# An FNet block on one core: the second DFT later behind its operand's turn, SyncE's stores and loads moved, other addresses for Z's halves, a later last sum

## The chip, the core and the metric

The kernel runs on one core of a Trainium2 chip. The metric is the device time of one execution in microseconds (us), lower is better; it is the median of several runs. Engines are named as the profile names them: PE (TensorE, matmuls; PEld is its weight load), DVE (VectorE), ACT (ScalarE), POOL (GpSimd) and SP (SyncE, which in this kernel issues every DMA, in the order in which they are written).

## What is computed

Two sublayers with pre-normalization, on x of 2048 tokens by 448 channels, all in float32:

```python
x = A_x                                              # 1 x 2048 x 448
a = einsum("bsd,ed->bse", layernorm(x), dft_hid_re)  # DFT over channels
b = einsum("bsd,ed->bse", layernorm(x), dft_hid_im)
h = x + einsum("ts,bse->bte", dft_seq_re, a) - einsum("ts,bse->bte", dft_seq_im, b)
n = layernorm(h)
g, u = n @ w_gate, n @ w_up                          # 448 x 1792 each
out = h + (gelu(g) * u) @ w_down                     # 1792 x 448
```

## The kernel before, in words

Every float32 operand is split into two float16 halves (a high part, and a low part that is the rest), and each product is three matmuls: high by high, high by low, low by high. The high part is made on ACT (line 104), the low part on DVE (lines 108 and 110).

*The first stage: the DFT over the sequence.* The order of the two DFTs is turned round: the sequence comes first. For a pair p of token tiles (0 to 7, two groups g of 128 tokens, real and imaginary part), Z is a sum over 16 tiles of the normalized x, collected in PSUM banks acc (line 443). Pairs 0 and 1 run together in steps 0 to 15; from step 16 on each of the pairs 2 to 7 takes eight steps. A step n is 24 matmuls in all cases. `seq_load(n + 5)` loads raw DFT weights wr five steps ahead (lines 394, 399), and ACT and DVE make their halves ws three steps ahead.

*Z's way to the second DFT.* When a sum is done, `z_out` (line 453) makes its halves zs, two buffers, on ACT and DVE. `z_turn(p)` (line 462) issues four transposing DMAs on SP from zs to z, of which there is one buffer. `hid_mm(p, g)` (line 503) is the second DFT: 21 matmuls on z into y, in the one bank of the pool ps_tr, and then on DVE the sum of y into h, in the tile hx, which `h_tile` has filled with x. `h_store` writes hx to DRAM.

*What else goes on in that stage.* Pairs 0 to 3 of h are already made into operands of the next stage: moments and norm (`ffn_stats`, `ffn_norm`), sums (`ffn_sums`), halves xs, one buffer (`ffn_split`), and four transposing DMAs to hops (`ffn_transpose`, line 284). The gate and up weights are made into halves for 14 blocks f, one block every three steps: two loads into raw (two buffers, line 303), sums, two splits, and a store to DRAM (line 336).

*What sets the order.* All of this is written out by hand in two tables: `early[n]` holds what is issued in step n ahead of its matmuls, `after[n, half]` what is issued behind the first or the second half of step n's matmuls. Each engine takes its own instructions in the order in which they are written, and waits at the first one whose data or buffer isn't ready. So a store in SP's queue that waits for DVE holds back every load and every transpose written after it. In SBUF a new pool lies where a closed one was, and its tiles wait for what last used the addresses.

*The second stage: gate and up.* It opens when the last Z is done. Its pool fpool lies where the first stage's tiles were. A block t of `GateUp` has three banks X, Y, Z; `open` makes X and Y, from X ACT makes u1 (line 809), DVE u2 from Y and u1, and so on (`plus`, line 781). The last turn, z of pair 7, is issued in front of the stage, and `hid_mm(7, g)` runs at the ends of blocks 2 and 3, with DVE's sum and moments behind it. Blocks 3 to 6 take their weights from a tile gw_first, loaded from DRAM at the start of the stage (line 662). Down weights wd are prepared on ACT, DVE and POOL, one half block to a block t. The third stage, with the down projection, isn't touched.

Of the kernel before, what the change touches and what calls it, by code (L numbers as in the profile page):

```python
# [8 lines left out]
F16 = mybir.dt.float16  # L9
F32 = mybir.dt.float32  # L10
# [22 lines left out]
def kernel(  # L33
# [140 lines left out]
    def ffn_moments(q, j, h, g):  # L174
        tag = f"h{q}_{j}"
        if g == 0:
            moments[q, j] = const.tile([P, 2, 2], F32, tag=f"mv_{tag}", name=f"mv_{tag}")
        st = small.tile([P, 6], F32, tag="st", name=f"st_{tag}_{g}")
        V.bn_stats(st, h[:, g, :])
        V.bn_aggr(moments[q, j][:, g, :], st)  # L180
# [6 lines left out]
    def ffn_stats(q, j, h):  # L187
        for g in range(2):
            ffn_moments(q, j, h, g)
        ffn_rstd(q, j)  # L190
# [16 lines left out]
    def ffn_norm(q, j, h):  # L207
        tag = f"h{q}_{j}"
        mv, r = moments.pop((q, j))
        xn = fops.tile([P, 2, D], F32, tag="xn", name=f"xn_{tag}")  # L210
        for g in range(2):
            normed(xn[:, g, :], h[:, g, :], mv, r, g)
        ffn[q, j] = xn
# [12 lines left out]
    def ffn_sums(q, j, parts=range(4)):  # L226

        if 0 in parts:
            t = fops.tile([P, 960], F32, tag="tt", name=f"tt_{q}_{j}")
            ffn[q, j] = ffn[q, j], t  # L230
        xn, t = ffn[q, j][:2]
        sub = V.tensor_sub
        if 0 in parts:
            sub(t[:, 0:256], xn[:, 1, 0:256], xn[:, 0, 0:256])
        if 1 in parts:
            sub(t[:, 256:448], xn[:, 1, 256:448], t[:, 0:192])
            V.tensor_scalar(t[:, 448:512], t[:, 192:256], -1.0, None, op0=ALU.mult)
        if 2 in parts:
            sub(t[:, 512:704], xn[:, 1, 256:448], xn[:, 1, 0:192])
            V.tensor_scalar(t[:, 704:768], xn[:, 1, 192:256], -1.0, None, op0=ALU.mult)  # L240
        if 3 in parts:

            sub(t[:, 768:960], xn[:, 0, 256:448], t[:, 256:448])
# [31 lines left out]
    def ffn_split(q, j):  # L275
        ffn_hi(q, j)
        ffn_lo(q, j)

    def ffn_transpose(q, j, parts):
        xs = ffn[q, j][2]  # L280
        ops = hops[q]
        for n in parts:
            s0, s1 = ((0, 8), (8, 16), (16, 22), (22, 25))[n]
            nc.sync.dma_start_transpose(ops[:, s0:s1, j * P : (j + 1) * P], xs[:, s0 * P : s1 * P])  # L284
# [116 lines left out]
    def ws_tile(n):  # L401
        ws[n] = dft.tile([P, 2, 8 * P], F16, tag="ws", bufs=6, name=f"ws{n}")
# [5 lines left out]
    def seq_lo(n):  # L408
        lo_part(ws[n][:, 1], wr[n], ws[n][:, 0], D_SC)


    def first_load(c, jj):
        if c == 0:
            wr[jj] = dft.tile([P, 8 * P], F32, tag="wr", bufs=5, name=f"wr{jj}")
            ws_tile(jj)
        cols = slice(c * P, (c + 1) * P)
        nc.sync.dma_start(wr[jj].rearrange("p (b t) -> p b t", b=4)[:, :, cols], w_seq[8 * jj][:, :, cols])
# [30 lines left out]
                stop=c == NT - 1 and m == 2,  # L448
            )

    zs, z = {}, {}

    def z_out(p, part, g):
        if p not in zs:
            zs[p] = dft.tile([P, 2, 2, 2 * D], F16, tag="zs", bufs=2, name=f"zs{p}")
        sc = 1.0 / (X_SC * D_SC)
        ps = acc.pop((p, part, g))[:, :D]
        hi, lo = [zs[p][:, g, l, part * D : (part + 1) * D] for l in range(2)]
        hi_part(hi, ps, sc)
        lo_part(lo, ps, hi, sc)  # L460

    def z_turn(p):
        z[p] = hidp.tile([P, 2, 7, 2 * P], F16, tag="z", name=f"z{p}")
        for g in range(2):
            for l in range(2):
                nc.sync.dma_start_transpose(z[p][:, l, :, g * P : (g + 1) * P], zs[p][:, g, l, :])
# [32 lines left out]
    def h_tile(q, j):  # L499
        hp[q, j] = pair_tile(f"hx{q}_{j}")  # L500
        nc.sync.dma_start(hp[q, j], xr[q // 2, 2 * (q % 2) + j])

    def hid_mm(p, g):

        y = ps_tr.tile([P, 512], F32, tag="tr", name=f"y_{p}_{g}")
        for k in range(7):
            for m, (lz, lw) in enumerate(((0, 0), (0, 1), (1, 0))):
                PE.matmul(  # L508
                    y[:, :D],
                    z[p][:, lz, k, g * P : (g + 1) * P],  # L510
                    wh[:, lw, k, :],
                    start=k == 0 and m == 0,
                    stop=k == 6 and m == 2,
                )
        h = hp[p // 2, p % 2][:, g, :]
        V.scalar_tensor_tensor(h, y[:, :D], 1.0 / D_SC, h, op0=ALU.mult, op1=ALU.add)  # L516

    def h_store(q, j):
        nc.sync.dma_start(h_dram[2 * q + j], hp[q, j])
# [6 lines left out]
    def at(where, n, *what):  # L526
        where.setdefault(n, []).extend(what)
# [4 lines left out]

    for k, f in enumerate(reversed(range(NF))):
        n = 17 + 3 * k
        at(early, n - 4, lambda f=f: gu.update({f: Weights(f)}))
        at(early, n, lambda f=f: gu[f].sums())
        at(early, n + 1, lambda f=f: gu[f].split(True))
        at(early, n + 2, lambda f=f: gu[f].split(False), lambda f=f: gu[f].store())
    for p in range(NP - 1):
        b, j = divmod(p, 2)  # L540

        n = (16, 21)[p] if p < 2 else 8 * p + 8
        at(early, n - 1, lambda b=b, j=j: h_tile(b, j))
        at(after, (n, 0), lambda p=p: z_turn(p))
        for g in range(2):
            at(after, (n + 2 + g, 0), lambda p=p, g=g: hid_mm(p, g))
        at(early, n + 4, lambda b=b, j=j: ffn_stats(b, j, hp[b, j]))
        at(early, n + 4, lambda b=b, j=j: h_store(b, j))
        if b < 2:
            at(early, n + 4, lambda b=b, j=j: ffn_norm(b, j, hp[b, j]))  # L550
            at(early, n + 5, lambda b=b, j=j: ffn_sums(b, j))
            at(early, n + 6, lambda b=b, j=j: ffn_split(b, j))
            for k in range(4):
                at(after, (n + 7 + k // 2, k % 2), lambda b=b, j=j, k=k: ffn_transpose(b, j, (k,)))
    at(early, N_STEPS - 2, lambda: h_tile(NB - 1, 1))
    at(early, 50, lambda: down_load(0), lambda: down_load(1))
    at(early, 56, lambda: down_sums(0))
# [427 lines left out]
    def dn_ahead(t):  # L985

        if t in (NF - 4, NF - 1):
            dn_sums(int(t == NF - 1))
        if NF <= t < 6 * NC + 12:
            dn_sums(t - 12)  # L990
# [72 lines left out]
    for t in range(N_GU):  # L1063
        q, f = divmod(t, NF)
        if f == 0 and q < 3:
            hh[q] = fpool.tile([P, NC, 4, TQ], F32, tag="hh", bufs=2, name=f"hh{q}")
            if 1 <= q <= 2:
                hops_tile(q + 1)
        if 0 < t < 4:
            gw_load(t + 6)  # L1070
        elif 7 < t < N_GU - 2:
            gw_load(t + 2)
        if t == 3 * NF:
            last_begin()
            down_load(0)
            down_load(1)
        if q == 3:
            hq[t] = late.tile([P, 2, TQ], F32, tag="hq", bufs=2, name=f"hq{t}")
        d = t - NF
        if d >= 0 and d % NC == 1:  # L1080
            hr_load(d // NC)
        if t in (N_GU - 2, N_GU - 1):
            hr_load(t - N_GU + 8)
        cur.z_open()
        if t > 0:
            if q == 0:
                prev.c12_plus()
            prev.c_last()
        if t + 1 <= 2 * NC:
            down_prep(t + 1)  # L1090
        if q == 0:
            dn_ahead(t)
            cur.xy()
            if f == NF - 2:
                dn_split(0)
            prev = cur
            cur = GateUp(t + 1)
            cur.open()
            prev.yz()
            if t in (2, 3):  # L1100

                hid_mm(NP - 1, t - 2)
                ffn_moments(NB - 1, 1, hp[NB - 1, 1], t - 2)
            if t == 3:
                h_store(NB - 1, 1)
                ffn_rstd(NB - 1, 1)
                hid.close()
                late = ctx.enter_context(tc.tile_pool(name="late", bufs=1, reuse_waits="tile"))
            if d == -1:
                prev.c12_plus()  # L1110
            continue
        do(t, 0)
        if d + 1 < 6 * NC:
            dn_split(d + 1)
        dn_mm(d, range(0, 8))
        cur.xy()
        dn_ahead(t)
        dn_mm(d, range(8, 18))
        do(t, 1)
        do(t, 4)  # L1120
        cur.yz()
        cur.c12_plus()
        dn_mm(d, range(18, 21))
        do(t, 5)
        do(t, 2)
        do(t, 3)
        prev = cur
        if t + 1 < N_GU:
            cur = GateUp(t + 1)
            cur.open()  # L1130
# [101 lines left out]
```

## Time and profile before

| what | value |
|---|---|
| median of 3 runs | 741.06 us (740.93 to 741.16) |
| the profiled execution | 741.05 us |
| its span in the trace | 739.3 us |
| PE busy | 718.7 us, 97% of the span |
| matmuls of the sequence DFT, acc | 293.4 us busy |
| matmuls of the second DFT, y | 69.3 us busy |
| y's idle time in front of it | 9.8 us |
| mean granted PE clock | 0.991 |

A busy share says how long an engine had an instruction under way. The number in brackets at the end of a timeline row is the time for which the engine stood before it, and what ended that. SPq rows are SP's issues: their length is the time of issuing, not that of the transfer. x4 at a row's end says that four instructions were merged into it.

### The profile page before, as it was taken

To read this page: it belongs to the slowest core of one execution; us is meant where nothing else is said; L and a number is where in the kernel's file an instruction comes from. 1 tells how busy PE (TensorE), PEld (TensorE's weight loads), DVE (VectorE), ACT (ScalarE), POOL (GpSimd) and SP (SyncE) were. 2 spreads that over 40 slices of the span, in tenths; PEclk is the share of its full clock that TensorE was granted. 3 is DMA by queue.
4 is the path that set the end of the run, shared out by engine and by line. 5 is a ranking of instruction groups with operands and counts; after the bars stand their busy time and mean duration, and the time that the engine had idled before them with its cause. 6 is when DMAs were issued, how large, how long until landed. Compare 5 with 4: busy or idle time off the path is not lost.

```text
span 739.3 us, 13609 instructions
## 1 busy us (share of the span) xinstructions
PE 718.7 (97%) x5301; PEld 517.6 (70%) x5301; DVE 517.1 (70%) x1064; ACT 293.4 (40%) x564; POOL 236.5 (32%) x277
## 2 busy tenths in 40 slices
PE   9999999999599999999988999999999999999998
PEld 6555555555255455555566889999999999999998
DVE  6897548767259275562255787888788887888887
ACT  6775514334135133341133434343443433444321
POOL 0000000000000000100052876568586776867541
PEclk9999999999799999999999999999999999999999
DMA  7787568858959979494192364665747578475401
GB/s 262 246 249 267 137 204 226 213 186 244 240 211 289 226 248 321 165 282 140 36 370 93 127 224 176 179 191 165 204 176 214 181 160 263 154 245 209 165 26 51
DMA packets 100305, 147.20 MB, mean 199 GB/s; under 512 B 60816, under 2 KB 70160, under 8 KB 100240
## 3 DMA queue, kind: packets, MB, share of 16 engines
q1 hardware_dynamic: 100240, 146.34, 64.1%
q8 instruction: 41, 0.67, 0.4%
q14 instruction: 24, 0.20, 0.1%
HBM read 112.23 MB, written 20.19 MB: 179 GB/s over the span
## 4 chain that ended last, share of the span: by engine, by line
PE 88%; SPq 4%; DMA 3%; DVE 3%; ACT 1%; issue 1%; DVEq 0%; ACTq 0%
PE acc L443 32%; PE pY L771 14%; PE acc_d L719 11%; PE y L508 9%; PE pX L771 9%; PE pZ L771 9%; SPq L284 2%; PE last_a L976 2%; DMA x<-in_x_dram 1%; DMA z<-zs 1%; PE last_X L934 1%; PE last_tr L934 1%; SPq L303 1%; DVE ws L110 1%; DVE gu_w L110 0%
## 5 line engine op out<-in xcount | busy, mean ns | idle before, releaser
L443 PE MATMUL acc<-xs,ws 128*128 128x448 f16 x1536 | 293.4, 353 | 0.1
L443 PEld LDWEIGHTS <-ws 128*128 128x128 f16 x1536 | 150.4, 98 | 140.5 <-issue 0.6
L771 PEld LDWEIGHTS <-gw 128*128 128x128 f16 x1911 | 186.7, 98 | 19.4 <-issue 0.5
L202 POOL TENSOR_TENSOR wd_s<-wd 128x448 f32<-128x448 f32 x7 | 8.0, 1137 | 369.8 <-DMA wr<-in_w_seq_dram 296.0
L771 PE MATMUL pY<-hops,gw 128*128 128x256 f16 x833 | 114.0, 273 | 0.1
L719 PE MATMUL acc_d<-wd,dn_w 128*128 128x224 f16 x882 | 105.1, 259 | 0.0
L110 DVE SCALAR_TENSOR_TENSOR ws<-wr,ws 128x1024 f16<-128x1024 f32 (+1 forms) x66 | 78.4, 1190 | 21.2 <-ACT ws L104 20.8
L104 ACT ACTIVATE ws<-wr 128x1024 f16<-128x1024 f32 (+1 forms) x66 | 66.6, 1020 | 63.2 <-DMA wr<-in_w_seq_dram 61.9
L719 PEld LDWEIGHTS <-dn_w 128*128 128x128 f16 x882 | 85.0, 98 | 2.8
L508 PE MATMUL y<-wh,z 128*128 128x448 f16 x336 | 69.3, 362 | 9.8 <-DMA z<-zs 9.8
L771 PE MATMUL pX<-hops,gw 128*128 128x256 f16 x539 | 74.8, 273 | 0.0
L771 PE MATMUL pZ<-hops,gw 128*128 128x256 f16 x539 | 73.7, 273 | 0.0
L781 DVE SCALAR_TENSOR_TENSOR u<-pY,u 128x256 f32<-128x256 f32 x112 | 47.0, 419 | 31.4 <-ACT c L845 18.4
L508 PEld LDWEIGHTS <-z 128*128 128x128 f16 x336 | 33.2, 100 | 43.2 <-DMA z<-zs 11.9
L104 ACT ACTIVATE zs<-acc 128x448 f16<-128x448 f32 x32 | 17.2, 541 | 102.2 <-PE acc L443 92.8
L809 ACT ACTIVATE u<-pX 128x256 f32<-128x256 f32 x56 | 21.4, 382 | 85.7 <-PE pX L771 82.2
L108 DVE TENSOR_TENSOR dn_w<-dn_s,dn_w 128x640 f16<-128x640 f32 x42 | 52.6, 1253 | 1.5 <-ACT dn_w L104 1.2
L110 DVE SCALAR_TENSOR_TENSOR zs<-acc,zs 128x448 f16<-128x448 f32 x32 | 19.4, 623 | 48.1 <-ACT zs L104 48.0
L516 DVE SCALAR_TENSOR_TENSOR hx<-y,hx 128x448 f32<-128x448 f32 x16 | 10.0, 625 | 61.6 <-PE y L508 61.6
L822 ACT ACTIVATE g<-pX 128x256 f32<-128x256 f32 x56 | 21.4, 383 | 74.7 <-PE pX L771 66.5
L847 POOL TENSOR_TENSOR hh<-hh,c 128x256 f32<-128x256 f32 x42 | 39.3, 935 | 28.2 <-ACT c L845 28.1
L838 POOL TENSOR_TENSOR hh<-hh,g 128x256 f32<-128x256 f32 x42 | 30.9, 736 | 53.3 <-DVE hh L781 51.4
(117 smaller groups left out, 865.8 us busy)
## 6 DMA issues: line engine op xcount, KB each, us to landing
gw<-w_dram SPq DMA_DIRECT2D x49, 896.0 KB, 5.0
wr<-in_w_seq_dram SPq DMA_DIRECT2D x100, 256.0 KB, 5.0
w_dram<-gu_w SPq DMA_DIRECT2D x14, 896.0 KB, 4.9
gu_raw<-in_w_gu_dram SPq DMA_DIRECT2D x28, 384.0 KB, 5.9
wr<-in_w_seq_dram SPq DMA_DIRECT2D x14, 512.0 KB, 5.4
wd<-in_w_down_dram SPq DMA_DIRECT2D x14, 448.0 KB, 5.4
x<-in_x_dram SPq DMA_DIRECT2D x16, 224.0 KB, 3.1
hx<-in_x_dram SPq DMA_DIRECT2D x8, 448.0 KB, 5.7
```

Of the source, the lines that this page charges most:

```text
L104: A.activation(dst, src, AF.Copy, scale=scale)
L108: V.tensor_sub(dst, src, hi)
L110: V.scalar_tensor_tensor(dst, src, scale, hi, op0=ALU.mult, op1=ALU.subtract)
L443: PE.matmul(acc[key][:, :D], w[:, lw, block * P : (block + 1) * P], xs[c][:, lx, :], start=c == 0 and m == 0, stop=c == NT - 1 and m == 2,)
L508: PE.matmul(y[:, :D], z[p][:, lz, k, g * P : (g + 1) * P], wh[:, lw, k, :], start=k == 0 and m == 0, stop=k == 6 and m == 2,)
L719: PE.matmul(acc[k // 2][:, k % 2 * HD : (k % 2 + 1) * HD], a_of(la, a), b_of(lb, b), start=first and m == 0 and k % 2 == 0, stop=last and ...
L771: PE.matmul(ps, w[:, wl, wa + ws, :], ops[:, m + ms, :], start=first and n == 0, stop=last and n == len(terms) - 1, skip_group_check=True,)
L781: V.scalar_tensor_tensor(dst, ps, SC, other, op0=ALU.mult, op1=ALU.add)
L809: A.activation(self.u1, self.X, AF.Copy, scale=SC)
L822: A.activation(self.g1, self.X, AF.Gelu_apprx_tanh, scale=1.0 / (X_SC * W_SC))
L838: G.tensor_mul(c21, c21, self.g1)
L847: G.tensor_mul(c22, c22, self.c12)
```

## The change

The parts: (a) z_turn of pairs 0 to 6 stands behind steps 16, 20, 25, 32, 40, 48 and 56 (the second and third behind the second half); hid_mm starts in steps 19, 24, 29, 36, 44, 52 and 60, where it was 18, 23, 26, 34, 42, 50 and 58. (b) What hangs on hid_mm moves with it: hx's load, moments, h's store, norm, sums, halves and hops; for pair 3 the norm and what follows two steps more. (c) Loads of gate and up weights, their stores and h's stores go from `early` to `after`, behind half a step. (d) zs's two buffers are allocated at the first loads, ahead of ws. (e) hid_mm is split into matmuls and `hid_add`, and the last pair's two sums run a block later, behind DVE's work for that block; the square root moves to block 5.

```diff
     def first_load(c, jj):
         if c == 0:
             wr[jj] = dft.tile([P, 8 * P], F32, tag="wr", bufs=5, name=f"wr{jj}")
+            zs_tile(jj)
             ws_tile(jj)
...
     def z_out(p, part, g):
         if p not in zs:
-            zs[p] = dft.tile([P, 2, 2, 2 * D], F16, tag="zs", bufs=2, name=f"zs{p}")
+            zs_tile(p)
...
-        y = ps_tr.tile([P, 512], F32, tag="tr", name=f"y_{p}_{g}")
+        y = ys[p, g] = ps_tr.tile([P, 512], F32, tag="tr", name=f"y_{p}_{g}")
...
+    def hid_add(p, g):
         h = hp[p // 2, p % 2][:, g, :]
-        V.scalar_tensor_tensor(h, y[:, :D], 1.0 / D_SC, h, op0=ALU.mult, op1=ALU.add)
+        V.scalar_tensor_tensor(h, ys[p, g][:, :D], 1.0 / D_SC, h, op0=ALU.mult, op1=ALU.add)
...
-        at(early, n - 4, lambda f=f: gu.update({f: Weights(f)}))
+        at(after, (n - 4, 0), lambda f=f: gu.update({f: Weights(f)}))
         at(early, n, lambda f=f: gu[f].sums())
         at(early, n + 1, lambda f=f: gu[f].split(True))
-        at(early, n + 2, lambda f=f: gu[f].split(False), lambda f=f: gu[f].store())
-    for p in range(NP - 1):
+        at(early, n + 2, lambda f=f: gu[f].split(False))
+        at(after, (n + 3, 0), lambda f=f: gu[f].store())
+
+    turns = [(16, 0), (20, 1), (25, 1), (32, 0), (40, 0), (48, 0), (56, 0)]
+    for p, (n, half) in enumerate(turns):
         b, j = divmod(p, 2)
-        n = (16, 21)[p] if p < 2 else 8 * p + 8
-        at(early, n - 1, lambda b=b, j=j: h_tile(b, j))
-        at(after, (n, 0), lambda p=p: z_turn(p))
+        m = (19, 24, 29)[p] if p < 3 else n + 4
+        at(early, m - 1, lambda b=b, j=j: h_tile(b, j))
         for g in range(2):
-            at(after, (n + 2 + g, 0), lambda p=p, g=g: hid_mm(p, g))
-        at(early, n + 4, lambda b=b, j=j: ffn_stats(b, j, hp[b, j]))
-        at(early, n + 4, lambda b=b, j=j: h_store(b, j))
+            at(after, (m + g, 0), lambda p=p, g=g: hid_mm(p, g), lambda p=p, g=g: hid_add(p, g))
+        at(after, (n, half), lambda p=p: z_turn(p))
+        at(early, m + 2, lambda b=b, j=j: ffn_stats(b, j, hp[b, j]))
+        at(after, (m + 2, 0), lambda b=b, j=j: h_store(b, j))
         if b < 2:
-            at(early, n + 4, lambda b=b, j=j: ffn_norm(b, j, hp[b, j]))
-            at(early, n + 5, lambda b=b, j=j: ffn_sums(b, j))
-            at(early, n + 6, lambda b=b, j=j: ffn_split(b, j))
+            m += 2 if p == 3 else 0
+            at(early, m + 2, lambda b=b, j=j: ffn_norm(b, j, hp[b, j]))
+            at(early, m + 3, lambda b=b, j=j: ffn_sums(b, j))
+            at(early, m + 4, lambda b=b, j=j: ffn_split(b, j))
             for k in range(4):
-                at(after, (n + 7 + k // 2, k % 2), lambda b=b, j=j, k=k: ffn_transpose(b, j, (k,)))
+                at(after, (m + 5 + k // 2, k % 2), lambda b=b, j=j, k=k: ffn_transpose(b, j, (k,)))
...
             dn_ahead(t)
+            if t in (3, 4):
+                hid_add(NP - 1, t - 3)
+                ffn_moments(NB - 1, 1, hp[NB - 1, 1], t - 3)
+            if t == 4:
+                h_store(NB - 1, 1)
             cur.xy()
...
             if t in (2, 3):
                 hid_mm(NP - 1, t - 2)
-                ffn_moments(NB - 1, 1, hp[NB - 1, 1], t - 2)
+            if t == 5:
+                ffn_rstd(NB - 1, 1)
             if t == 3:
-                h_store(NB - 1, 1)
-                ffn_rstd(NB - 1, 1)
                 hid.close()
```

SP's queue around the turn of pair 3 (steps 30 to 35; wrNN is the raw DFT weight of step NN, gu_raw and gu_w belong to the block that follows the name, hxQ_J and xs_Q_J to pair 2Q + J, z3 and zs3 to pair 3). Before:

```order
L284 DMA_TRANSPOSE hops0_160<-xs_0_1_1619 128x6x128
L284 DMA_TRANSPOSE hops0_160<-xs_0_1_1619 128x3x128
L399 DMA wr35_1787<-in_w_seq_dram 128x512 x2
L399 DMA wr36_1833<-in_w_seq_dram 128x512 x2
L336 DMA w_dram9_155<-gu_w9_1793 128x3584
L303 DMA gu_raw7_1844<-in_w_gu_dram 128x768 x2
L501 DMA hx1_1_1847<-in_x_dram 128x2x448
L284 DMA_TRANSPOSE hops1_161<-xs_1_0_1798 128x8x128 x2
L399 DMA wr37_1881<-in_w_seq_dram 128x512 x2
L284 DMA_TRANSPOSE hops1_161<-xs_1_0_1798 128x6x128
L466 DMA_TRANSPOSE z3_1905<-zs3_1642 128x7x128 x4
L284 DMA_TRANSPOSE hops1_161<-xs_1_0_1798 128x3x128
```

And in the changed kernel:

```order
L284 DMA_TRANSPOSE hops0_160<-xs_0_1_1635 128x6x128
L284 DMA_TRANSPOSE hops0_160<-xs_0_1_1635 128x3x128
L399 DMA wr36_1796<-in_w_seq_dram 128x512 x2
L303 DMA gu_raw7_1838<-in_w_gu_dram 128x768 x2
L528 DMA h_dram2_140<-hx1_0_1646 128x896
L399 DMA wr37_1858<-in_w_seq_dram 128x512 x2
L336 DMA w_dram9_155<-gu_w9_1742 128x3584
L471 DMA_TRANSPOSE z3_1889<-zs3_1606 128x7x128 x4
L399 DMA wr38_1906<-in_w_seq_dram 128x512 x2
L399 DMA wr39_1952<-in_w_seq_dram 128x512 x2
L303 DMA gu_raw6_1974<-in_w_gu_dram 128x768 x2
L284 DMA_TRANSPOSE hops1_161<-xs_1_0_1917 128x8x128 x2
```

z3 stood behind three of pair 2's four transposes (hops1 from xs_1_0) and behind pair 3's hx; now it stands ahead of them, and the weights of a later step follow the store instead of preceding it.

ACT at the opening of the gate and up stage, with what each instruction waits for (DMAHW are DMA completions). Before:

```order
L104 ACTIVATE zs7_3171<-acc7_11_3212 128x448 [waits PE_49]
L104 ACTIVATE wd0_3343<-wd32_0_2736 128x448
L104 ACTIVATE wd0_3343<-wd_s_0_3030 128x1120 [waits Pool_49]
L809 ACTIVATE u1_0_3379<-pX_0_3365 128x256 [waits DMAHW1_49,DMAHW2_49,DMAHW0_49,DMAHW7_49,DVE_49,PE_49]
L822 ACT_TABLE_LOAD
```

And in the changed kernel:

```order
L104 ACTIVATE zs7_3147<-acc7_11_3166 128x448 [waits PE_49]
L104 ACTIVATE wd0_3343<-wd32_0_2733 128x448
L104 ACTIVATE wd0_3343<-wd_s_0_3027 128x1120 [waits Pool_49]
L823 ACTIVATE u1_0_3379<-pX_0_3365 128x256 [waits PE_49]
L836 ACT_TABLE_LOAD
```

The order is the same; u1 of block 0 no longer waits for any DMA.

DVE around block 4 of that stage (hx3_1 and y_7_1 belong to the last pair). Before:

```order
L781 SCALAR_TENSOR_TENSOR hh0_3383<-pY_3_3543,u1_3_3556 128x256
L516 SCALAR_TENSOR_TENSOR hx3_1_3280<-y_7_1_3661,hx3_1_3280 128x448
L179 BN_STATS st_h3_1_1_3684<-hx3_1_3280 128x6
L180 BN_AGGR mv_h3_1_3595<-st_h3_1_1_3684 128x2
L132 RECIPROCAL r_h3_1_3690<-sd_h3_1_3688 128x2
```

And in the changed kernel:

```order
L795 SCALAR_TENSOR_TENSOR hh0_3383<-pY_3_3543,u1_3_3556 128x256
L795 SCALAR_TENSOR_TENSOR c12_3_3694<-pZ_3_3596,u2_3_3558 128x256
L110 SCALAR_TENSOR_TENSOR wd2_3345<-wd_s_2_3522,wd2_3345 128x1120
L525 SCALAR_TENSOR_TENSOR hx3_1_3279<-y_7_1_3661,hx3_1_3279 128x448
L179 BN_STATS st_h3_1_1_3706<-hx3_1_3279 128x6
L180 BN_AGGR mv_h3_1_3611<-st_h3_1_1_3706 128x2
L795 SCALAR_TENSOR_TENSOR u3_4_3723<-pY_4_3632,u1_4_3645 128x256
```

c12 of block 3 and the low part of wd block 2 stood behind the sum and the root; now they stand ahead of the sum, and the root follows a block later.

More of the change, by code (lines that the diff above doesn't have):

```diff
@@ L409, in seq_lo, with zs_tile @@
         lo_part(ws[n][:, 1], wr[n], ws[n][:, 0], D_SC)
+    zs, z = {}, {}
+    def zs_tile(p):
+        zs[p] = dft.tile([P, 2, 2, 2 * D], F16, tag="zs", bufs=2, name=f"zs{p}")
     def first_load(c, jj):
@@ L449, in seq_mm @@
             )
-    zs, z = {}, {}
     def z_out(p, part, g):
         if p not in zs:
-            zs[p] = dft.tile([P, 2, 2, 2 * D], F16, tag="zs", bufs=2, name=f"zs{p}")
+            zs_tile(p)
         sc = 1.0 / (X_SC * D_SC)
@@ L501, in h_tile @@
         nc.sync.dma_start(hp[q, j], xr[q // 2, 2 * (q % 2) + j])
+    ys = {}
     def hid_mm(p, g):
-        y = ps_tr.tile([P, 512], F32, tag="tr", name=f"y_{p}_{g}")
+        y = ys[p, g] = ps_tr.tile([P, 512], F32, tag="tr", name=f"y_{p}_{g}")
         for k in range(7):
```

## The prediction

> **What bounds the kernel now.** I read the page first, then the waits of the TensorE, then its timeline around each wait, then the queues that the waits point to.
>
> ```profile
> span 739.3 us, 13609 instructions
> PE 718.7 (97%) x5301; PEld 517.6 (70%) x5301; DVE 517.1 (70%) x1064; ACT 293.4 (40%) x564; POOL 236.5 (32%) x277
> PEclk9999999999799999999999999999999999999999
> ...
> PE y L508 <- DMA z<-zs: 9.8, 4, 7.8
> PE pX L771 <- ACT u L809: 3.9, 1, 3.9
> PE pY L771 <- DVE u L781: 2.3, 2, 1.4
> ```
>
> The TensorE (PE) is busy 97% of the span, so only what it waits for, and what it runs slowly after a wait, can be won. Beside the start there are three sources: the hidden DFT's product y waits for z, the first gate/up product waits for ScalarE's u1, and two later ones wait for VectorE. The one slice at clock 7 says that a wait also costs slow matmuls after it. So I measure each loss in the timeline, from the regular end of the work before to the start of the work behind.
>
> ```profile
> 155.63 31.94 PE L443 MATMUL acc<-xs,ws 128*128 128x448 f16 x168
> 195.39 0.93 PE L508 MATMUL y<-wh,z 128*128 128x448 f16 x2 [7.81 <-DMA z<-zs]
> 196.61 6.11 PE L508 MATMUL y<-wh,z 128*128 128x448 f16 x19 [0.29 <-DMA z<-zs]
> 202.56 4.70 PE L443 MATMUL acc<-xs,ws 128*128 128x448 f16 x24
> ...
> 211.07 31.94 PE L443 MATMUL acc<-xs,ws 128*128 128x448 f16 x168
> 244.42 0.55 PE L508 MATMUL y<-wh,z 128*128 128x448 f16 x2 [1.40 <-DMA z<-zs]
> 245.22 3.77 PE L508 MATMUL y<-wh,z 128*128 128x448 f16 x19 [0.25 <-DMA z<-zs]
> 248.82 4.70 PE L443 MATMUL acc<-xs,ws 128*128 128x448 f16 x24
> 253.36 4.14 PE L508 MATMUL y<-wh,z 128*128 128x448 f16 x21
> 257.34 31.94 PE L443 MATMUL acc<-xs,ws 128*128 128x448 f16 x168
> 289.12 4.14 PE L508 MATMUL y<-wh,z 128*128 128x448 f16 x21
> 293.09 4.70 PE L443 MATMUL acc<-xs,ws 128*128 128x448 f16 x24
> ```
>
> The last four rows are the undisturbed rhythm: a step of 24 matmuls takes 253.36 - 248.82 = 4.54 us, seven steps 289.12 - 257.34 = 31.78, a y 293.09 - 289.12 = 3.97. For pair 3, seven steps from 155.63 end at 187.41 and y should end at 191.38. The next step starts at 202.56: **11.18 us lost**. For pair 4, 211.07 + 31.78 + 3.97 = 246.82 against 248.82: **2.00 us lost**. Pairs 0 to 2, 5 and 6 lose nothing: these waits are all that the trace has.
>
> Why z is late is read from SyncE's queue (SP), which issues every DMA in order, and from ScalarE (ACT).
>
> ```profile
> 162.08 0.33 SPq L336 DMA_DIRECT2D w_dram<-gu_w  x1
> 164.68 5.33 SPq L284 DMA_TRANSPOSE hops<-xs  x2
> 171.15 2.53 SPq L284 DMA_TRANSPOSE hops<-xs  x2
> 175.21 0.83 ACT L104 ACTIVATE xs<-xn_h 128x256 f16<-128x256 f32 x2 [8.63 <-DMA hops<-xs]
> 181.01 0.33 SPq L336 DMA_DIRECT2D w_dram<-gu_w  x1
> 184.30 4.88 SPq L284 DMA_TRANSPOSE hops<-xs  x2
> 191.64 5.45 SPq L466 DMA_TRANSPOSE z<-zs  x4
> ```
>
> z of pair 3 belongs behind the first half of step 32, at 155.63 + 5 x 4.54 = 178.3. It leaves at 191.64. A weight store stood until 162.08 for its data; behind it pair 1's transposes went late; ACT, which refills their single source buffer xs for pair 2, stood 8.63 us for them; and the store of step 31, which needs what VectorE (DVE) does behind that, left only at 181.01. Pair 2's transposes came next, then z. So this is a queue that trips over its own waits, two pairs' FFN operands being made within three steps of each other.
>
> **The change part by part.** No engine gets an instruction more or less; the TensorE's sum of work stays, and so does each DMA.
>
> *(1) y four steps behind the turn instead of two (pairs 3 to 6; 3 to 4 instead of 2 for pairs 0 to 2).* Up to 187.41 the TensorE had lost nothing, so y of pair 3 now falls due at 187.41 + 2 x 4.54 = 196.5. If z left SP exactly as late as before, its last half would be there at 196.61: a wait of 0.1 us. Upper end of the price: for pair 4 the TensorE comes 11.18 us earlier than before and two steps later, at 242.85 - 11.18 + 9.08 = 240.75; if z4 came at its old absolute time, 245.22, that would be 4.5 us. But z4 was late for a like reason (pair 3's hops transposes just ahead of it), and in the order now these stand behind it. I take 0 for both. Gain: 11.18 + 2.00 = **13.18 us**, with a loss of up to 4.5 us kept for the range.
>
> *(2) SP's order.* FFN operands of pairs 0 to 3 are normalized at steps 21, 26, 31 and 40 instead of 20, 25, 28 and 36; the third pair no longer comes three steps behind the second, and its transposes stand behind z3. Weight stores and h stores go out behind half a step of matmuls, so the loads of that step no longer stand behind them. The price is on hx: its load comes only one step ahead of the step in whose middle y starts, where it was three. The rows are the page's part on DMA issues, SP's waits (total, times, longest) and the view of tile hx.
>
> ```profile
> hx<-in_x_dram SPq DMA_DIRECT2D x8, 448.0 KB, 5.7
> SPq L336 <- DVE gu_w L110: 62.0, 8, 13.7
> L516 DVE SCALAR_TENSOR_TENSOR hx<-y,hx x16: 624/625/625, 95.1 to 399.4; 128x448 f32<-128x448 f32 x16
> ```
>
> hid_add of the first half is due 1.5 x 4.54 + 3.97 = 10.8 us after the load's turn; the load takes 5.7, which leaves 5.1. The TensorE itself waits only where the single bank of y isn't free for the second half, 4.54 - 0.62 = 3.9 us later: 9.0 us of lateness are covered. The worst wait of SP for a store is 13.7, but much of such a wait is SP having run ahead. I take 0; the uncovered end is the rival below.
>
> *(3) Other addresses for zs.* zs is now placed before the first ws, and u1 of the gate/up stage no longer lies on it. ACT's u1 and DVE's u2 lose their waits for the last four transposes; what lies there now is wd of blocks 4 and 5, needed some 30 us later.
>
> ```profile
> 366.50 0.54 ACT L104 ACTIVATE zs<-acc 128x448 f16<-128x448 f32 x1 [1.73 <-PE acc L443]
> 367.40 1.13 ACT L104 ACTIVATE wd<-wd_s 128x1120 f16<-128x1120 f32 x1
> 367.61 0.82 PE L771 MATMUL pZ<-hops,gu_w 128*128 128x256 f16 x6
> 371.93 0.38 ACT L809 ACTIVATE u<-pX 128x256 f32<-128x256 f32 x1 [3.40 <-DMA z<-zs]
> 372.36 1.23 PE L771 MATMUL pX<-hops,gu_w 128*128 128x256 f16 x5 [3.94 <-ACT u L809]
> 375.72 1.36 PE L771 MATMUL pY<-hops,gu_w 128*128 128x256 f16 x11
> 378.12 0.71 PE L771 MATMUL pX<-hops,gu_w 128*128 128x256 f16 x5
> 379.98 1.26 PE L771 MATMUL pY<-hops,gu_w 128*128 128x256 f16 x10
> ```
>
> The three openings should end at 367.61 + 0.65 = 368.26; the 17 matmuls behind them take 379.98 - 378.12 = 1.86 in rhythm but end at 375.72, so 375.72 - 368.26 - 1.86 = 5.60 us are lost, 3.94 waiting and the rest slow. Without the wait, ACT still has its two wd conversions ahead of u1: free at 367.40 + 1.13 = 368.53, u1 done at 368.91, the TensorE goes on at some 368.96. Left over: 0.70 us. Gain: **4.9 us**; at the ends 0 (another wait takes its place) and 5.6.
>
> The granted clock falls where the TensorE stood long: after 7.81 us pair 3's y lost another 11.18 - 7.81 - 0.29 = 3.08 us, after 3.94 us the opening lost 1.66. The Trainium skill (TensorE: Matmul & The Clock Gate, Part 1) has the array at half clock after an idle window of some 3.4 us, and at full clock again after some 3.4 busy ones, which as an estimate is 1.7 us for each cold start. The opening agrees with that; pair 3 does not, and by the page the gain of part 1 would be 1.4 us smaller. I hold to the rows.
>
> *(4) The last pair's sum into h later.* In the gate/up stage DVE stood in front of y, with the work of the next two blocks behind it.
>
> ```profile
> 390.16 0.62 DVE L516 SCALAR_TENSOR_TENSOR hx<-y,hx 128x448 f32<-128x448 f32 x1 [4.09 <-PE y L508]
> 394.09 0.71 PE L771 MATMUL pY<-hops,gw_first 128*128 128x256 f16 x5 [0.81 <-DVE u L781]
> 403.92 0.71 PE L771 MATMUL pY<-hops,gw_first 128*128 128x256 f16 x5 [1.44 <-DVE u L781]
> 394.47 1.28 ACT L125 ACT_TABLE_LOAD   x1
> ```
>
> c12 and wd's low part now run in the 4.09 us in which DVE stood; the add comes when y is there. Gain 0.81 + 1.44 = **2.25 us**. The root and its two table loads, 2 x 1.28 us on ACT, move to block 5; block 5 has no wd conversion ahead of them and the TensorE needs some 4.3 us for a block, so I expect them hidden, and 1.4 us if not (the longest such wait now).
>
> Sum: 13.18 + 4.9 + 2.25 = 20.3 us. The profiled execution took 741.05 us around its span of 739.3, and the runs' median is 741.06, so both bases are one: **741.05 - 20.3 = 720.7 us**.
>
> **Rivals.**
> *z still late, or something else of the DFT stage.* For it: during 180 to 210 the DMAs are busy too, and the time won for the TensorE is taken from the others. The rows give a stretch's bounds and length, the busy time of PE, PE's weight load, DVE, ACT and POOL, the granted clock, the DMA share and GB/s.
>
> ```profile
> 180.00:210.00 30.00, 21.89 (x102) 10.25 (x100) 13.55 (x22) 6.28 (x9) 0.00 (x0) 0.83 0.94 267
> 260.00:370.00 110.00, 108.42 (x581) 56.74 (x580) 55.48 (x100) 34.11 (x53) 2.83 (x3) 1.00 0.63 199
> ```
>
> With 0.94 of the DMAs in use, a transpose may land late however it is queued. Against it: the stage's other stretches are lower (0.63 from 260 on), and nothing is added. Price: from the 4.5 us of part 1 up to pair 3's whole 11.2: 725.2 to 731.9 us.
>
> *The opening waits for something else.* The weights of blocks 3 to 6 are reloaded right behind the last turn.
>
> ```profile
> L662 SPq DMA_DIRECT2D gw_first<-w_dram x4: 422/480/842, 370.1 to 371.7; - x4
> DMA to landing us min/median/max: 5.4/7.8/10.4
> 383.58 0.82 PE L771 MATMUL pX<-hops,gw_first 128*128 128x256 f16 x6
> ```
>
> The rows are the view of tile gw_first and the TensorE's timeline. The first block was used from 383.58 on, which becomes some 378.7. If the first load is the quickest, it is there at 370.1 + 5.4 = 375.5 and nothing waits; if it took the 10.4, at 380.5, 1.9 us go. If the whole of part 3 failed, 4.9. Time 722.6 to 725.6 us.
>
> *Slower: hx.* SP's lateness at a pair's hx load goes over 9.0 us, DVE stands in hid_add, the one bank of y isn't freed and the TensorE stands at each y's second half. At the full 13.7 us of SP's longest store wait that is 4.7 us for a pair, for seven pairs 33: 741.05 - 20.3 + 33 = 753.6 us. It is slower than before once the lateness is over 9.0 + 20.3 / 7 = 11.9 us at every pair. Against it: stores now stand behind the hx loads of their step.
>
> *The change doesn't do what it says:* the waits only move to the later y and to wd, 741 us; against it stand the addresses and the 0.1 us of part 1.
>
> **How the numbers follow.** Forecast 0.65; z or the DFT stage 0.18; the opening 0.11; no change 0.02; slower 0.04. The range: below, the 0.7 us left over and up to 1 us of small waits might go too, 719.0; above, it takes in the opening's rival and the nearer half of the DFT one, 728.5. That leaves out the far half (0.09), no change and slower, some 0.15. About 0.2% (1.5 us) is what a measurement of this kernel can tell from no change. Faster 0.94, same 0.02, slower 0.04.
>
> **What would show it.** Right: among the TensorE's waits no row for z, or one under 0.5 us; all y runs of 21 in 4.1 us; no slice with clock 7; from the last acc to the next gate/up matmul under 1 us; no wait of pY for u in the first six blocks; span near 719. Wrong: a y row with a wait for z or for hx's add (step 1 or 2), ACT's first u waiting for a DMA (3), a wait for gw_first at block 3 or for ACT around the square root at block 5 (4).

## The result, and the profile after

The changed kernel takes 720.62 us (720.31 to 720.93) where the kernel before, run beside it, takes 741.11: a ratio of 0.9725, 95% interval 0.9712 to 0.9737. The prediction was 720.7. Single executions that took 3% or more above the median of the others of the same kernel, one in each of four runs below, are left out of all medians and ratios here.

The page after, its first rows, and then the TensorE's waits (us in total, times, longest):

```profile
span 719.1 us, 13629 instructions
PE 712.8 (99%) x5301; PEld 515.6 (72%) x5301; DVE 517.4 (72%) x1064; ACT 293.8 (41%) x564; POOL 236.6 (33%) x277
...
PEclk9999999999999999999999999999999999999999
```

```profile
PE pw L98 <- POOL sign_t L89: 1.4, 1, 1.4
PE acc L450 <- DVE xs L108: 0.7, 2, 0.4
PE acc L450 <- ACT xs L364: 0.6, 1, 0.6
PE pX L785 <- ACT u L823: 0.4, 1, 0.4
```

No wait of y for z is left, none of pY for u, and the slice at clock 7 is gone. Of u1's wait 0.4 us remain. The waits of acc for xs lie in the first steps and make 1.3 us here; in the runs below that change only later steps they make 0.3 to 1.2 us.

The TensorE's timeline after, around y of pairs 3 and 4 and around the opening of the gate and up stage:

```profile
196.82 4.13 PE L515 MATMUL y<-wh,z 128*128 128x448 f16 x21
200.79 4.70 PE L450 MATMUL acc<-xs,ws 128*128 128x448 f16 x24
...
241.09 4.14 PE L515 MATMUL y<-wh,z 128*128 128x448 f16 x21
245.06 4.70 PE L450 MATMUL acc<-xs,ws 128*128 128x448 f16 x24
...
353.45 0.82 PE L785 MATMUL pX<-hops,gu_w 128*128 128x256 f16 x6
...
356.01 0.71 PE L785 MATMUL pX<-hops,gu_w 128*128 128x256 f16 x5 [0.43 <-ACT u L823]
...
357.86 1.36 PE L785 MATMUL pY<-hops,gu_w 128*128 128x256 f16 x11
```

Both y run in 3.97 us. Before, the first pX of the stage stood here:

```profile
366.30 0.82 PE L771 MATMUL pX<-hops,gu_w 128*128 128x256 f16 x6
```

Three stretches account for the whole difference of the spans. From the start to the first pX: 366.30 before, 353.45 now, 12.85 us. From there to the pY of eleven matmuls: 375.72 - 366.30 = 9.42 before, 357.86 - 353.45 = 4.41 now, 5.01 us. The rest: 363.58 before, 361.24 now, 2.34 us. Sum 20.20, which is 739.3 - 719.1. Predicted were 13.18, 4.9 and 2.25.

SyncE's queue after, around the turn of pair 3:

```profile
155.67 8.68 SPq L284 DMA_TRANSPOSE hops<-xs  x2
...
165.77 2.57 SPq L284 DMA_TRANSPOSE hops<-xs  x2
...
172.77 0.48 SPq L336 DMA_DIRECT2D w_dram<-gu_w  x1
175.01 7.96 SPq L471 DMA_TRANSPOSE z<-zs  x4
...
186.84 5.49 SPq L284 DMA_TRANSPOSE hops<-xs  x2
```

z3 begins to leave at 175.0 where it was 191.6, and the issue is over at 183.0. The y that reads it starts at 196.8. So there are some 14 us between, of which the two steps of added distance are only 9.1: at its old place y would most likely have found z there too (a z transpose of this run takes 3.1 us from issue to landing in the median). That is the first sign that the largest term had another cause than the one predicted.

### The profile page after: what moved, and what is told of

Read it like the earlier page. It is cut to its first block, busy times and chain, and to the rows that moved or that the text cites. A ratio compares the mean times of both kernels' runs of the same rounds, so it can differ in the third digit from the quotient of the medians.

```text
span 719.1 us, 13629 instructions
## 1 busy us (share of the span) xinstructions
PE 712.8 (99%) x5301; PEld 515.6 (72%) x5301; DVE 517.4 (72%) x1064; ACT 293.8 (41%) x564; POOL 236.6 (33%) x277
## 4 chain that ended last, share of the span: by engine, by line
PE 95%; DMA 2%; DVE 1%; ACT 1%; issue 0%; DVEq 0%
PE acc L450 39%; PE pY L785 14%; PE acc_d L733 12%; PE pZ L785 9%; PE pX L785 9%; PE y L515 9%; PE last_a L990 2%; DMA x<-in_x_dram 2%; PE last_X L948 1%; PE last_tr L948 1%; ACT wd L104 0%; PE last_Y L990 0%; DVE c L795 0%; ACT L125 0%; DVE st_x L118 0%
## 5 line engine op out<-in xcount | busy, mean ns | idle before, releaser
L515 PE MATMUL y<-wh,z 128*128 128x448 f16 x336 | 66.2, 352 | 0.0
L110 DVE SCALAR_TENSOR_TENSOR zs<-acc,zs 128x448 f16<-128x448 f32 x32 | 19.5, 623 | 48.2 <-ACT zs L104 48.2
```

The source lines that it names most:

```text
L110: V.scalar_tensor_tensor(dst, src, scale, hi, op0=ALU.mult, op1=ALU.subtract)
L515: PE.matmul(y[:, :D], z[p][:, lz, k, g * P : (g + 1) * P], wh[:, lw, k, :], start=k == 0 and m == 0, stop=k == 6 and m == 2,)
```

## The experiments

### Which part brings the 13 us of the sequence DFT

Two theories. *Distance*: z is late, and y four steps behind the turn covers it. *Order*: with SP's queue in its new order z isn't late, and the distance isn't needed. Within the second, three things could be the cause: the pairs' FFN dates, as the prediction had it, the stores, or the loads.

**The distance taken away.** In the changed kernel:

```diff
-        at(early, m - 1, lambda b=b, j=j: h_tile(b, j))
+        y = m - 2 if p >= 3 else m
+        at(early, y - 1, lambda b=b, j=j: h_tile(b, j))
         for g in range(2):
-            at(after, (m + g, 0), ...
+            at(after, (y + g, 0), ...
```

> The changed kernel with y of pairs 3 to 6 (and hx's load) two steps earlier again, two steps behind the turn; all else, SP's order of turns, hops transposes and stores above all, as changed. If the order of SP's queue is the cause of the late z: z3 leaves SP at 175 us as in the changed kernel and is there by some 183 to 185, y would be due at 196.8 - 9.1 = 187.7; z4 leaves at 219.2, there by 228, due at 232.0. No wait, 720.6 us, within 0.7. If the distance is what makes up for a late z: the 11.2 and 2.0 us come back, up to 733.8 us.

Measured: 720.47 us, ratio to before 0.9726 (0.9705 to 0.9747). Its timeline of SP and of the TensorE:

```profile
174.67 5.79 SPq L471 DMA_TRANSPOSE z<-zs  x4
...
218.81 5.26 SPq L471 DMA_TRANSPOSE z<-zs  x4
```

```profile
187.40 4.14 PE L515 MATMUL y<-wh,z 128*128 128x448 f16 x21
...
231.66 4.14 PE L515 MATMUL y<-wh,z 128*128 128x448 f16 x21
```

z3 has left by 180.5 and y starts at 187.4 without a wait. For pairs 3 to 6 the distance brings nothing here.

**The distance alone.** In the kernel before, ahead of the loop over g:

```diff
+        n += 2 if p >= 3 else 0
         for g in range(2):
             at(after, (n + 2 + g, 0), lambda p=p, g=g: hid_mm(p, g))
```

> The kernel before with y of pairs 3 to 6, and what depends on it, two steps later; nothing else. If a late z is only covered by distance: z3 leaves SP as late as before (191.6 us) and its last half comes at 196.6, y is due at 196.5; pairs 3 and 4 lose nothing or next to it: 741.1 - 13.2 = 727.9 us. If the queue's lateness goes on behind that: pair 4 waits up to 4.5 us, 732.4 us. If the distance does nothing: 741.1 us.

Measured: 737.4 us (four times, 736.0 to 738.1), ratio 0.9956 (0.9935 to 0.9977). That is 3 us of the 13, and none of the three expectations. The same kernel was run once more, for its timeline.

> The kernel before with y of pairs 3 to 6, and what depends on it, two steps later, once more, for its profile; the first four undisturbed times had a median of some 737.4 us, where the prediction's step 1 makes 727.9. If the time is still lost at y: z3 comes as late as before or later, waits of y for z of 8 us and more in sum. If y waits no more: a new wait of some 9 us elsewhere in the DFT stage, of acc for ws or of y for DVE.

Measured: 736.46 us beside 740.64, ratio 0.9948 (0.9931 to 0.9964). The TensorE, then SP, ACT and DVE in that run:

```profile
196.04 4.14 PE L508 MATMUL y<-wh,z 128*128 128x448 f16 x21
200.02 4.70 PE L443 MATMUL acc<-xs,ws 128*128 128x448 f16 x24
210.86 5.62 PE L508 MATMUL y<-wh,z 128*128 128x448 f16 x21 [6.14 <-DVE hx L516]
216.32 31.94 PE L443 MATMUL acc<-xs,ws 128*128 128x448 f16 x168
```

```profile
191.37 5.29 SPq L466 DMA_TRANSPOSE z<-zs  x4
...
198.01 2.00 SPq L399 DMA_DIRECT2D wr<-in_w_seq_dram  x4
```

```profile
203.09 1.06 ACT L104 ACTIVATE ws<-wr 128x1024 f16<-128x1024 f32 x1 [7.74 <-DMA wr<-in_w_seq_dram]
```

```profile
204.18 1.23 DVE L110 SCALAR_TENSOR_TENSOR ws<-wr,ws 128x1024 f16<-128x1024 f32 x1 [7.41 <-ACT ws L104]
...
210.19 0.62 DVE L516 SCALAR_TENSOR_TENSOR hx<-y,hx 128x448 f32<-128x448 f32 x1
```

z3 leaves as late as before, and the first half of y starts at 196.04 without a wait: so far the expected picture. But the DFT weights wr stand behind z3 in SP's queue. ACT waits 7.74 us for them, DVE 7.41 us for ACT, and the sum of y into h, which comes behind that in DVE's order, runs at 210.19. Until then the one bank of y isn't free, and the second half, due at 200.02 + 4.54 = 204.56, waits 6.14 us. The next run of acc starts at 216.32 instead of 208.53: 7.8 us lost, where the same pair lost 11.2 before. The distance moves the wait from z to the bank of y; what is late is the queue.

**The FFN dates alone.** In the kernel before:

```diff
         if b < 2:
+            n += (0, 0, 3, 4)[p]
             at(early, n + 4, lambda b=b, j=j: ffn_norm(b, j, hp[b, j]))
```

> The kernel before with norm, sums, halves and hops transposes of pair 2 three steps and of pair 3 four steps later (the dates of the changed kernel); y, the stores and the addresses as before. If the pairs' spacing is the cause: pair 1's transposes are done before ACT wants to fill xs again, no wait of ACT for hops, z3 stands ahead of pair 2's transposes and leaves near 182, 741.1 - 13.2 = 727.9 us, with a microsecond or two more where a store still holds the queue. If the stores are the cause: 739 to 742 us.

Measured: 732.66 us beside 740.34, ratio 0.9898 (0.9868 to 0.9929): 7.7 us. SP and the TensorE:

```profile
161.68 0.33 SPq L336 DMA_DIRECT2D w_dram<-gu_w  x1
...
164.29 5.36 SPq L284 DMA_TRANSPOSE hops<-xs  x2
...
177.57 0.33 SPq L336 DMA_DIRECT2D w_dram<-gu_w  x1
...
181.44 8.27 SPq L466 DMA_TRANSPOSE z<-zs  x4
```

```profile
188.86 0.55 PE L508 MATMUL y<-wh,z 128*128 128x448 f16 x2 [1.68 <-DMA z<-zs]
189.66 3.77 PE L508 MATMUL y<-wh,z 128*128 128x448 f16 x19 [0.25 <-DMA z<-zs]
...
234.11 0.55 PE L508 MATMUL y<-wh,z 128*128 128x448 f16 x2 [0.39 <-DMA z<-zs]
235.83 3.77 PE L508 MATMUL y<-wh,z 128*128 128x448 f16 x19 [1.17 <-DMA z<-zs]
```

With pair 2's transposes out of its way z3 leaves 10 us earlier, and y waits 1.9 and 1.6 us for pairs 3 and 4. But the store still stands until 161.7 and pair 1's transposes leave as late as before. The dates are a part of the cause, not the whole.

**Stores and loads alone**, then **the weight stores alone**, both in the kernel before. The first has all of this diff, the second only the three lines with `split(False)` or `store()`:

```diff
-        at(early, n - 4, lambda f=f: gu.update({f: Weights(f)}))
+        at(after, (n - 4, 0), lambda f=f: gu.update({f: Weights(f)}))
-        at(early, n + 2, lambda f=f: gu[f].split(False), lambda f=f: gu[f].store())
+        at(early, n + 2, lambda f=f: gu[f].split(False))
+        at(after, (n + 3, 0), lambda f=f: gu[f].store())
-        at(early, n + 4, lambda b=b, j=j: h_store(b, j))
+        at(after, (n + 4, 0), lambda b=b, j=j: h_store(b, j))
```

The weight loads and h's stores move by half a step. A weight store moves by one and a half steps, here as in the change: from ahead of step n + 2's matmuls to behind the first half of step n + 3's. In SP's queue it lets pass, among others, the loads of one step and the transposes that are due behind the two halves of step n + 2.

> The kernel before with the loads of gate and up weights, their stores and h's stores half a step later; y, the FFN operands and the addresses as before. If the stores that stand in SP's queue are the cause: z3 leaves near 180 us, 741.1 - 13.2 = 727.9 us. If the cause is that pair 2's operands are made three steps behind pair 1's, and their transposes stand ahead of z3: ACT still stands for the hops transposes, z3 leaves near 190, 739 to 742 us.

> The kernel before with nothing but the stores of the gate and up weights half a step and a step's loads later (one line). If these stores are what holds SP's queue: pair 1's hops transposes leave without the wait until 162, ACT stands for them next to nothing, z3 leaves near 180, 728 us. If the weight loads or h's stores are needed for it: over 732 us.

Measured: 728.09 us, ratio 0.9832 (0.9813 to 0.9850), and 728.6 us, ratio 0.9837 (0.9816 to 0.9857). Moving the weight stores brings 12.0 of the 13 us; what the loads and h's stores add, 0.5 us, lies within the intervals. SP, ACT and the TensorE with the stores alone moved:

```profile
156.66 4.11 SPq L284 DMA_TRANSPOSE hops<-xs  x2
...
162.00 0.38 SPq L336 DMA_DIRECT2D w_dram<-gu_w  x1
...
181.52 6.79 SPq L466 DMA_TRANSPOSE z<-zs  x4
```

```profile
168.56 0.83 ACT L104 ACTIVATE xs<-xn_h 128x256 f16<-128x256 f32 x2 [2.22 <-DMA hops<-xs]
```

```profile
187.16 4.41 PE L508 MATMUL y<-wh,z 128*128 128x448 f16 x21
191.41 4.70 PE L443 MATMUL acc<-xs,ws 128*128 128x448 f16 x24
```

The store itself leaves at 162.0, just as before (162.08). But pair 1's first two transposes now stand ahead of it and leave at 156.7 instead of 164.7; ACT waits 2.2 us for them instead of 8.6, its work and DVE's behind it come earlier, and z3 leaves ten microseconds earlier although it still stands behind pair 2's transposes. y loses 4.25 - 3.97 = 0.3 us. So the cause is shown: a store written into SP's queue while its data were still being made, with everything of the next step behind it. All 14 weight stores moved in this run; that it is the one at 162 us that counts is read from the timeline.

### The two smaller terms, each undone in the changed kernel

zs allocated where it was (the line `zs_tile(jj)` in first_load left out):

> The changed kernel with zs allocated where it was, so that u1 of the gate and up stage lies on it again. If part 3 was read rightly: ACT's first u waits for the last turn's transposes, PE stands 3.9 us and is slow after it, 720.6 + 4.9 = 725.5 us. If the other parts took that wait away already (the last transposes earlier, say): 720.6 us.

Measured: 725.39 us, ratio 0.9787 (0.9772 to 0.9801), 4.8 us more than the changed kernel. The opening in its profile, ACT's first u and then the TensorE:

```profile
358.54 0.38 ACT L822 ACTIVATE u<-pX 128x256 f32<-128x256 f32 x1 [3.38 <-DMA z<-zs]
```

```profile
354.24 0.82 PE L784 MATMUL pZ<-hops,gu_w 128*128 128x256 f16 x6
358.97 0.71 PE L784 MATMUL pX<-hops,gu_w 128*128 128x256 f16 x5 [3.92 <-ACT u L822]
...
360.83 1.36 PE L784 MATMUL pY<-hops,gu_w 128*128 128x256 f16 x11
```

The wait is back, and it is for the last turn's transposes. In this one execution (723.95 us) the matmuls behind it ran at their usual speed; the three others, 1.3 to 2.0 us longer, show a mean granted clock of 0.998 instead of 1.0.

The last pair's sums, moments, store and root back in blocks 2 and 3:

```diff
-            if t in (3, 4):
-                hid_add(NP - 1, t - 3)
-                ffn_moments(NB - 1, 1, hp[NB - 1, 1], t - 3)
-            if t == 4:
-                h_store(NB - 1, 1)
...
                 hid_mm(NP - 1, t - 2)
-            if t == 5:
-                ffn_rstd(NB - 1, 1)
+                hid_add(NP - 1, t - 2)
+                ffn_moments(NB - 1, 1, hp[NB - 1, 1], t - 2)
             if t == 3:
+                h_store(NB - 1, 1)
+                ffn_rstd(NB - 1, 1)
```

> The changed kernel with the last pair's sums, moments, store and root back where they were in blocks 2 and 3. If part 4 was read rightly: PE waits for u 0.8 and 1.4 us again, 720.6 + 2.3 = 722.9 us. If what ran earlier in the stage had made these waits go: 720.6 us.

Measured: 722.86 us, ratio 0.9755 (0.9743 to 0.9768), 2.2 us more than the changed kernel, and among its waits

```profile
PE pY L785 <- DVE u L795: 2.2, 2, 1.4
```

### The price of the later loads of x

```diff
-        at(early, m - 1, lambda b=b, j=j: h_tile(b, j))
+        at(after, (m, 0), lambda b=b, j=j: h_tile(b, j))
```

> The changed kernel with the load of x into hx behind the first half of y's own step, right ahead of y, instead of one step ahead of that step. The load takes 5.7 to 6.0 us, y 3.97: DVE stands some 2 us in the first hid_add of each pair. If 9.0 us of lateness are covered (this uses 1.5 steps, 6.8, of them): no PE wait, 720.6 us, within 0.7. If the rival of a slower kernel is near: PE stands at y's second half or at ws, 1 us or more for each of seven pairs, 728 us or more.

Measured: 721.0 us (720.1, 721.0, 722.2), ratio 0.9732 (0.9715 to 0.9748). The view of tile hx, then the one pair for which the TensorE waited, on SP, DVE and PE:

```profile
DMA hx<-in_x_dram: 19.5, 4
```

```profile
157.88 1.35 SPq L506 DMA_DIRECT2D hx<-in_x_dram  x1
```

```profile
166.17 0.62 DVE L525 SCALAR_TENSOR_TENSOR hx<-y,hx 128x448 f32<-128x448 f32 x1 [7.24 <-DMA hx<-in_x_dram]
```

```profile
166.85 4.13 PE L515 MATMUL y<-wh,z 128*128 128x448 f16 x21 [1.52 <-DVE hx L525]
```

DVE stood for x four times, 19.5 us in all and not the 2 us a pair that were expected, and once that reached the TensorE. The edit moves the load by 1.5 steps, 6.8 us; with 9.0 us covered none should have come through. The sum took the load to leave on time and to take 5.7 us. For the pair that waited it left at 157.88, 1.2 us behind its turn (y, which is written right behind it, starts at 156.65), and landed 8.2 us after its issue, 2.5 more. That is 3.7 us, as the wait has it: 9.0 - 6.8 + 1.5 = 3.7. The changed kernel itself shows no wait of DVE for x.

### u1 ahead of the down weights, and the parts put together

In the changed kernel `down_prep(0)` moved from ahead of the opening of block 0 to behind it:

> The changed kernel with the first half block of down weights prepared behind the opening of block 0 instead of ahead of it, so that ACT makes u1 before its two wd conversions. The wait of 0.43 us for u1, 0.6 us with its fringe, goes: 720.0 us. If the conversions then hold back g1 or u1 of block 1: no gain, or up to 1.7 us slower.

Measured: 719.95 us (719.52 to 720.26), ratio 0.9715 (0.9702 to 0.9727). The wait is gone:

```profile
354.63 0.82 PE L785 MATMUL pZ<-hops,gu_w 128*128 128x256 f16 x6
355.29 0.71 PE L785 MATMUL pX<-hops,gu_w 128*128 128x256 f16 x5
```

It is the fastest kernel of the study, 0.7 us under the changed one; the intervals of the two ratios overlap, the times of the two do not.

Then the kernel before with the three parts that brought something and nothing else of the change: the weight stores, zs's place, the later sums; and the same with `down_prep(0)` moved. (zs is allocated just ahead of wr there, in the change just behind it; u1 waits for no DMA in either.)

> The kernel before with three edits of the change alone: the weight stores half a step and a step's loads later, zs at the first loads, the last pair's sums and root later. y two steps behind the turn, the FFN dates, the weight loads, h's stores and hx as before. If these three carry all of it: 12.0 + 4.8 + 2.3 = 19.1 us less than before, 721.5 us, within 1 of the changed kernel. If the dates and the distance are needed once the other waits have gone: a wait of y for z again, 724 us or more.

> The same three edits, and the first half block of down weights prepared behind the opening of block 0. If the gain of this edit is its own: 0.5 us less than the run with the three edits alone, 721.0 us. If the changed kernel's dates matter: slower than 722 us.

Measured: 720.79 us (720.50 to 720.94), ratio 0.9713 (0.9685 to 0.9741), and 720.28 us (719.86 to 720.76), ratio 0.9708 (0.9684 to 0.9731). With the three parts alone one trace of the old order is left, in the TensorE's waits:

```profile
PE y L514 <- DMA z<-zs: 0.4, 2, 0.2
```

Three parts give the whole gain within what can be told apart. The distance, the FFN dates, the later weight loads, h's later stores and the later loads of x aren't needed for it. Moving `down_prep(0)` takes 0.5 us more off the median here, with times that overlap. What the stores' old place would cost in the changed kernel, with the new dates and the distance kept, was not run.

## Why the prediction was right, and where it was not

*The time and the three losses* were right: 11.18 + 2.00, 4.9 and 2.25 us were read from the TensorE's rhythm around each wait, and 12.85, 5.01 and 2.34 went. Measuring from the end of the work before to the start of the work behind counted the slow matmuls too, which the waits' own sum (9.8 us for z) does not.

*Step 1 was wrong in its cause.* It gave the 13.18 us to the distance, since y two steps later falls due at 196.5 and z came at 196.6. That sum was true of z (the first half of y does start at 196.0 in the run with the distance alone), and the run gained only 4.2 us, because the step asked only when z comes. What stood behind z in SP's queue was as late: wr, with it ACT and DVE, with them the one bank of y. Of the bounds kept there, 0 to 4.5 us for z4, neither held for what happened: 7.8 us at pair 3's second half. That the whole sum came out is luck in this term: it had the size of the loss right, but the loss went by other parts of the same change, of which the weight stores alone take 12.0 us, and it stays away with the distance undone. The distance alone made 736.5 us where the step makes 727.9.

*Step 2 had the gain and was priced at 0.* The reading of SP's queue ahead of the steps told the chain correctly, store, hops transposes, ACT's xs, the next store, z. But it took the pairs' dates for the root, and the dates alone bring 7.7 us, the store alone 12.0. The two aren't to be added: both shorten the same chain, at different places.

*Its price for hx* was too small a risk: 9.0 us were called covered by the median time of the load, and a shift of 6.8 us already came through once. The rival in which this makes the kernel slower didn't come about; in the changed kernel no sum waited for a load of x.

*Step 3* was right in mechanism and size, down to the remainder: 0.70 us were left by its sum, and 356.01 - 355.42 = 0.59 are there (the three openings end at 354.76 + 0.66). *Step 4* was right; the root with its two table loads in block 5 brought no wait of the TensorE.

*The rivals.* z late in another way didn't happen with all parts in place, and did in the run with the distance alone, as a wait for the bank. The opening didn't wait for gw_first: it was first used at 365.8, and the loads began at 357.25.

## What to carry to other kernels

In a queue that runs in the written order, look for the row that waits for data just being made, and for what is written behind it; to put that row later, here by one and a half steps, is cheap and can be worth more than giving its victims more time (12.0 us against 4.2). Where a late transfer is covered by a later consumer, ask what else in the same queue is as late, and which engine and which single buffer stand behind that. And a gain that fits the sum doesn't show the cause: undoing the part that was credited with it cost nothing here.

## What the runs showed of the hardware

The price of a wait in slow matmuls isn't a fixed one. After 7.8 us of waiting pair 3's y lost 3.1 us more, after 6.14 us in the run with the distance alone 7.79 - 6.14 = 1.65, after 3.93 to 3.94 us at the opening 1.7 to 1.8 (in the kernel before, and in the run with the weight stores alone), and after 3.92 us with zs's old place 0.2 in the profiled execution. The granted clock over the matmuls behind the wait goes with it: 0.58, 0.72, 0.57 and 0.53, and 1.00 in the last. The Trainium skill (TensorE: Matmul & The Clock Gate, Part 1) says that the activity window is free-running and the number of cold matmuls varies from run to run; that agrees with the openings, where waits of the same 3.9 us cost 1.7 to 1.8 or 0.2, while the 3.1 us are nearly twice the 1.7 us that its 3.4 us window makes as an estimate.
